# The last two steps' products of an FNet and GELU kernel in two rounds of 128 tokens

## The chip, the core and the metric

The kernel runs on one core of one Trainium2 chip. The metric is the device time of one execution in microseconds (us). The kernel before was run three times: 1854.57, 1856.98 and 1858.54 us, so its median is 1856.98 us. The profile shown here is of one further execution, which took 1857.67 us; the span that it shows, from the first to the last instruction, is 1855.9 us.

The core has five engines with queues of their own: TensorE (PE in the profile, with its weight loads shown as PEld), VectorE (DVE), ScalarE (ACT), GpSimd (POOL) and SyncE (SP). Each works through its instructions in the order in which they were put down. SP and ACT also issue the DMA transfers of this kernel.

## What is computed

```python
def _attn_ref(x):                       # x: (8, 3008, 256) float32
    X = np.fft.fft(x, axis=1)
    X = np.fft.fft(X, axis=2)
    return X.real.astype(np.float32)

def _moe_ref(x, w_in, w_out):           # x: (24064, 256), w_in: (256, 2048), w_out: (2048, 256)
    h = x @ w_in
    g = h * (1.0 / (1.0 + np.exp(-1.702 * h)))
    return (g @ w_out).astype(np.float32)
```

The real part of a two-dimensional Fourier transform of each of the 8 sequences is the input of a two-layer network with a sigmoid GELU. The sequences count 3008 positions of 256 features; the network turns every position (a token) into 2048 hidden values and back into 256.

## The kernel before, in words

The transform along the 3008 = 47 x 64 positions is done in two stages of products with cosine and sine tables, after folding the input on its symmetry; the transform along the features is folded into the first weight matrix (`wcs`). What is left for a token is a pair of products, one with the cosine and one with the sine half, and their sum and difference give the hidden values of a token and of its mirror image at once.

The main loop runs over `steps`, which are tuples of sequence `b` (8), block `blk` (3), half `hh` (2) and step `p` (8, called `NP`). The eight steps of one `(b, blk, hh)` are a group: it deals with 256 pairs of tokens, and each step adds the share of 2 x 128 hidden values to the group's output sums. In a turn `t` of the loop the hidden values of step `t` are made (products on PE into the banks `x`, the activation on ACT, sums on DVE and POOL), and `product(t - LAG, ...)` with `LAG = 3` multiplies those of three steps earlier with the second weight matrix. The program's order on each engine is written out by hand; no planner changes it.

The second product uses a scheme with seven products instead of eight (Strassen's, in Winograd's form) over 2 x 2 blocks: two halves of the hidden values by two halves of the output features, for the token and for its mirror. In the groups between the first and the last, four of the seven are split in the same way once more (`deep(t)`). In the last group, `t >= last`, all seven products are taken whole. Their sums stand in four PSUM banks of 512 columns, of which columns 0 to 255 and 256 to 511 belong to two products: `pot[0]` (bank `o0`), `pot[1]` (bank `o1`), `pot[3]` (bank `po3`) and `pot[2]` (bank `low`, one product only).

Every product is issued by `halves` (line 184 is its matmul) as two instructions, one for the output's partitions 0 to 63 and one for 64 to 127. In the profile each of these fp32 instructions shows as two MATMUL records and two weight loads. The small products of the deep groups are issued at line 678, with 128 columns each.

For the last two steps of the whole program `product` does not issue at once. It keeps the plan of the second last step and then issues the two steps' products interleaved, bank by bank: 4 products into `o0`, 4 into `o1`, 4 into `po3` and 2 into `low`, each with all 256 columns. These are 14 products, 28 instructions and 56 records on PE, and nothing comes behind them there.

Then `combine` closes the group. ACT copies the first product's sum out of `o0` (line 747). DVE adds up the others in SBUF, in `oc` (lines 750, 751, 761 and 756), and `turned` transposes each half (half 0 is the tokens, half 1 their mirror images), 128 x 512 values, into the output tile `os` (line 730). After each of the two transposes `store` issues four DMAs of 64 KB, one for each 32 partitions, in runs of 64 values, which are 256 bytes (line 816). In the last group two of the four are issued by SP and two by ACT; elsewhere all are issued by SP. The group's sums on DVE in order are:

```python
c12 = c11 + pot[0][256:]        # L750, after ACT's copy of c11 = pot[0][:256]
c21 = c12 + pot[1][:256]        # L751
c12, c22' = c12, c21 + pot[1][256:]   # L761, one instruction of 512 columns
c11 += pot[3][:256]; c12 += pot[3][256:]   # L756, then transpose and store of half 0
c21 += pot[2][:256]             # L756, then transpose and store of half 1
```

(The third line stands for one addition into `oc[256:512]` and `oc[512:768]`.)

Of the kernel before, what the change touches and what calls it, by code (L numbers as in the profile page):

```python
# [29 lines left out]
ALU = mybir.AluOpType  # L30
# [10 lines left out]
RUN = 32  # L41
# [5 lines left out]
def view(ap, offset, *dims):  # L47
    return bass.AP(ap.tensor, ap.offset + offset, [list(d) for d in dims])


def free(ap, offset, *dims):
    return bass.AP(ap.tensor, ap.offset + offset, [list(ap.ap[0])] + [list(d) for d in dims])


def kp(u, a):

    n, i = a // 4, 2 * (a % 4) + u
    return 8 * n + i if n else 7 - i
# [54 lines left out]
def kernel(ctx: ExitStack, tc, x, w_in, w_out, tab1, tab2, out):  # L113
    nc = tc.nc
# [12 lines left out]
    op = ctx.enter_context(tc.tile_pool(name="op", bufs=2, space=SB))  # L127
# [25 lines left out]
    big = cv.tile([128, 19 * 1024], F32, tag="big", name="big")  # L153
# [15 lines left out]
    def bank(name, tag=None):  # L169
        if tag is None:  # L170
            tag = spare.pop(0)
            spare.append(tag)
        if tag in ("o0", "o1"):
            return o_banks[int(tag[1])]
        return (rest if tag[0] == "o" else psp).tile([128, 512], F32, tag=tag, name=name)
# [5 lines left out]
    def halves(out, lhs, rhs, **how):  # L181

        for c0 in (0, 64):
            nc.tensor.matmul(out[c0:c0 + 64], lhsT=lhs[:, c0:c0 + 64], rhs=rhs, skip_group_check=True, **how)  # L184
# [323 lines left out]
    NP = NF // 2  # L508
    steps = [(b, blk, hh, p) for b in range(B) for blk in range(NBLK) for hh in range(2) for p in range(NP)]
    vb, ht, xb, gt, pot = {}, {}, {}, {}, {}  # L510
    LEFT, MADE, RIGHT, SUM, RES, OUT = 0, 4096, 8192, 14336, 16384, 18432
    A11, A21, S3, S2 = range(4)
    A12, S4, A22, S1 = range(4)
    oc = big[:, OUT:OUT + 1024].rearrange("p (q n) -> p q n", q=4)
    last = len(steps) - NP

    def width(t):

        return 226 if steps[t][1:3] == (0, 1) else 256
# [26 lines left out]
    def left(t, q, n):  # L546
        return big[:, at_left(t, q):at_left(t, q) + n]

    def right(t, q, n):
        return big[:, at_right(t, q):at_right(t, q) + n]  # L550
# [74 lines left out]
    def deep(t):  # L625

        return NP <= t < last
# [20 lines left out]
    def spot(pair_, k):  # L648
        return 256 + 128 * pair_ if k == 1 else 768 * pair_ + 128 * SPOT[k]

    def both(k, *dims):
        return free((o_banks[1] if k == 1 else pot["low"])[:], spot(0, k), [spot(1, k) - spot(0, k), 2], *dims)
# [37 lines left out]
    def product(t, lo, hi):  # L690

        p, n = steps[t][3], width(t)
        if lo == 0 and p == 0:
            for q in range(2):
                pot[q] = bank(f"po{q}", f"o{q}")
            if t >= NP:
                pot[2] = pot["low"]
            if t >= last:
                pot[3] = bank("po3", "b2")
        if t < NP:  # L700

            h = ht[t]
            plan = [(half, dh, wo[:, p, 2 * f + dh, :], h[:, half, f, :n])
                    for half in range(2) for dh in range(2) for f in range(2)]
        else:
            plan = [(0, 0, wo[:, p, 0, :], left(t, A11, n)), (0, 1, wt[:, p, 0, :], left(t, S2, n)),
                    (1, 0, wt[:, p, 1, :], left(t, S3, n))]
            if not deep(t):
                plan += [(1, 1, wt[:, p, 3, :], right(t, S1, n)), (3, 1, wo[:, p, 3, :], right(t, S4, n)),
                         (3, 0, wo[:, p, 2, :], right(t, A12, n)), (2, 0, wt[:, p, 2, :], right(t, A22, n))]  # L710
        todo = plan[lo:hi]

        if t >= len(steps) - 2:
            if hi:
                return
            pot[t] = plan
            if t == len(steps) - 2:
                return
            todo = [it for pair_ in zip(pot.pop(t - 1), pot.pop(t)) for it in pair_]
        begun = set() if p else pot.setdefault("begun", set())  # L720
        for q, i, lhs, rhs in todo:
            halves(pot[q][:, i * 256:i * 256 + n], lhs, rhs, start=(p == 0 and q not in begun), stop=(p == NP - 1))
            begun.add(q)
        if hi is None and p == 0:
            del pot["begun"]

    def turned(t, o, half, src):

        b, blk, hh, p = steps[t]
        nc.vector.transpose(free(o[:], half * 512, [32, 2], [64, 8], [1, 32]), free(src, (RUN - 1) * half, [256, 2], [RUN, 8], [1 - 2 * half, RUN]))  # L730
        store(b, blk, hh, o, half)

    def combine(t):

        b, blk, hh, p = steps[t]
        if p < NP - 1:
            return
        n = width(t)
        o = pot["out"] = op.tile([128, 4, 256], F32, tag="os", name="os")
        if t < NP:  # L740
            for half in range(2):
                turned(t, o, half, pot[half][:])
            return
        if n < 256:
            nc.gpsimd.memset(oc[:, :, n:], 0.0)
        c11, c12, c21, c22 = (oc[:, q, :n] for q in range(4))
        nc.scalar.copy(c11, pot[0][:, 0:n])
        if deep(t):
            nc.scalar.copy(free(big[:], RES + 1024 + 384, [512, 2], [1, n // 2]), both(1, [1, n // 2]))
        nc.vector.tensor_tensor(c12, c11, pot[0][:, 256:256 + n], op=ALU.add)  # L750
        nc.vector.tensor_tensor(c21, c12, pot[1][:, 0:n], op=ALU.add)  # L751
        if deep(t):
            return
        fifth(free(pot[1][:], 256, [0, 2], [1, n]), n)
        for out_, i1, half in (c11, pot[3][:, 0:n], None), (c12, pot[3][:, 256:256 + n], 0), (c21, pot[2][:, 0:n], 1):
            nc.vector.tensor_tensor(out_, out_, i1, op=ALU.add)  # L756
            if half is not None:
                turned(t, o, half, oc[:, 2 * half:])

    def fifth(m5, n):  # L760
        nc.vector.tensor_tensor(free(oc, 256, [512, 2], [1, n]), oc[:, 1:3, :n], m5, op=ALU.add)  # L761
# [37 lines left out]
    def turn_last(t, half):  # L799

        if group_end(t):
            turned(t, pot["out"], half, oc[:, 2 * half:])

    def store(b, blk, hh, o, half):

        last = (b, blk, hh) == (B - 1, NBLK - 1, 1)
        k0, step = kp(0, 4 * blk), kp(1, 4 * blk) - kp(0, 4 * blk)
        row, by = (NA * (1 + RUN * (1 - hh)) - k0, -step) if half else (NA * RUN * hh + k0, step)
        for q in range(4):
            src = o[32 * q:32 * q + 32, 2 * half:2 * half + 2, :].rearrange("p i n -> p (i n)")  # L810
            eng = nc.scalar if last and q % 2 else nc.sync

            def put(at, k2s, places):
                dst = view(out, (b * S + row + at * by) * D + 64 * q, [NA * D, k2s], [by * D, places], [1, 64])
                part = src[0:k2s, 64 * at:64 * (at + places)]
                eng.dma_start(out=dst, in_=part.rearrange("p (n c) -> p n c", c=64))


            whole = 8 if blk or (hh == 0 and half == 0) else 7
            put(0, RUN, whole)  # L820
            if whole == 7 and (hh, half) != (1, 1):
                put(7, 1 if hh else RUN - 1, 1)
# [106 lines left out]
    n = len(steps)  # L929
# [52 lines left out]
    for t in range(n + LAG):  # L982
        if t < NP:
# [15 lines left out]
            if t >= LAG and t != LAG + 1:  # L999
                product(t - LAG, 0, None)  # L1000
            if t == LAG:
                product(1, 0, None)
# [16 lines left out]
        else:  # L1019
# [14 lines left out]
            if opening:  # L1034
                small_products(*other)
            cut = 0 if opening and not after else 3 if after else 2
            product(t - LAG, 0, cut)
            if after:
                small_products(one[0], one[1][:1])
# [27 lines left out]
        if t >= LAG:  # L1067
            combine(t - LAG)
            combine_last(t - LAG - 2)
            turn_last(t - LAG - 3, 0)  # L1070
            turn_last(t - LAG - 4, 1)
# [32 lines left out]
```

## Time and profile before

| what | value |
|---|---|
| median of three runs | 1856.98 us (1854.57 to 1858.54) |
| profiled execution | 1857.67 us, span 1855.9 us |
| PE busy | 1838.7 us, 99% of the span |
| DVE, ACT, POOL busy | 1514.7, 1151.2 and 971.2 us |
| granted TensorE clock | 0.999 over the span |
| last group of PE records (last two steps) | starts at 1843.91 us, last ends at 1850.12 us |
| last DVE instruction (the second transpose) | 1851.14 to 1851.85 us |
| last DMA packets | between 1854.4 and 1854.6 us |

The profile's page gives busy times and the chain of work that ended last. Its timeline lists instructions in order of time, merged where they are of one kind: start, time until the last of them ended, engine, line, operation, output and inputs, and how many. Records of PE overlap, because matmuls are pipelined; the pace of PE is read from the starts of two neighbouring groups, divided by the number of records. The view by stretches of time gives, for each stretch, the busy time of each engine, the granted clock, the busy share of the DMA engines and what they moved in GB/s.

### The profile page before, as it was taken

Reading aid. Unit: us, or ns where it says so; the run is one execution under the profiler, and the core shown is the slowest. Engines: PE = TensorE matmul, PEld = TensorE weight load, DVE = VectorE, ACT = ScalarE, POOL = GpSimd, SP = SyncE. Lnnn points to the kernel's source line nnn. Section 1 sums busy time; section 2 is a strip of 40 time slices with the busy share of each in tenths; the row PEclk is TensorE's granted clock in tenths of the full one; section 3 lists DMA queues with packets and bytes.
Section 4 is the critical chain, followed back from the end, with each engine's and each line's share of the span. In section 5 each row is a group of like instructions: output and inputs, shape, how many; then the busy total and the mean of one; then the engine's idle time right before and its main releaser. Section 6 shows DMA issues by size and latency. Waiting matters only on the chain.

```text
span 1855.9 us, 56072 instructions
## 1 busy us (share of the span) xinstructions
PE 1838.7 (99%) x23722; PEld 1401.5 (76%) x23722; DVE 1514.7 (82%) x2112; ACT 1151.2 (62%) x2241; POOL 971.2 (52%) x1053
## 2 busy tenths in 40 slices
PE   8999999999999999999999999999999999999998
PEld 4677777777777777777777777777777777778776
DVE  6988778888788877987789878888888888878874
ACT  5756666666666656666566666666666666656663
POOL 4776446744367434773348633476445754434442
PEclk9999999999999999999999999999999999999999
DMA  8821340215012340223302132121411111100111
GB/s 265 196 61 34 84 68 19 72 49 102 19 38 53 73 84 13 51 50 88 59 13 64 45 86 53 18 75 35 103 30 24 36 46 36 30 19 13 23 20 24
DMA packets 149706, 105.31 MB, mean 57 GB/s; under 512 B 106057, under 2 KB 130665, under 8 KB 148896
## 3 DMA queue, kind: packets, MB, share of 16 engines
q1 hardware_dynamic: 146624, 99.68, 23.7%
q8 instruction: 187, 3.06, 0.7%
q10 hardware_dynamic: 2832, 2.05, 0.5%
q14 instruction: 63, 0.52, 0.1%
HBM read 64.41 MB, written 48.05 MB: 61 GB/s over the span
## 4 chain that ended last, share of the span: by engine, by line
PE 90%; DVE 5%; ACT 3%; DMA 1%; issue 1%; DVEq 0%; ACTq 0%
PE x L184 33%; PE o L184 26%; PE low L678 23%; PE o L678 4%; PE ps L255 2%; DVE big L644 2%; PE ps L365 1%; DVE big L779 1%; PE psw L184 1%; DMA xt<-in_x_dram 1%; DVE big L604 1%; ACT x L585 1%; DVE big L622 0%; DMA small<-in_tab_dram 0%; ACT g L597 0%
## 5 line engine op out<-in xcount | busy, mean ns | idle before, releaser
L615 POOL TENSOR_TENSOR big<-big 128x256 f32<-128x256 f32 (+1 forms) x376 | 352.0, 936 | 828.7 <-ACT big L607 676.9
L184 PE MATMUL x<-pq,wcs 128*64 128x256 f32 (+1 forms) x6016 | 769.0, 376 | 1.9 <-ACT g L597 1.6
L644 DVE TENSOR_TENSOR big<-big 128x512 f32<-128x512 f32 (+1 forms) x736 | 618.9, 855 | 23.1 <-PE low L678 4.7
L184 PE MATMUL o<-big,wo 128*64 128x256 f32 (+1 forms) x4800 | 620.8, 375 | 0.1
L184 PEld LDWEIGHTS x<-pq,wcs 128*64 128x64 f32 x6016 | 412.2, 137 | 186.1 <-issue 15.0
L184 PEld LDWEIGHTS o<-big,wo 128*64 128x64 f32 x4800 | 341.8, 137 | 147.8 <-DVE big L622 0.5
L597 ACT ACTIVATE g<-x 128x512 f32<-128x512 f32 (+1 forms) x376 | 221.7, 590 | 369.9 <-PE x L184 368.6
L604 DVE TENSOR_TENSOR big<-g,x 128x512 f32<-128x512 f32 (+1 forms) x376 | 249.9, 665 | 212.8 <-ACT big L600 212.6
L585 ACT ACTIVATE x<-nb,af 128x256 f32<-128x256 f32 (+1 forms) x752 | 352.9, 469 | 76.2 <-DVE pq L372 63.1
L678 PE MATMUL low<-big 128*64 128x128 f32 (+1 forms) x5888 | 382.9, 270 | 0.0
L678 PEld LDWEIGHTS low<-big 128*64 128x64 f32 x5888 | 337.6, 137 | 29.2
L616 POOL TENSOR_TENSOR big<-big 128x256 f32<-128x256 f32 (+1 forms) x376 | 351.5, 935 | 0.0
L600 ACT ACTIVATE big<-x 128x512 f32<-128x512 f32 (+1 forms) x376 | 219.2, 583 | 128.2 <-PE x L184 122.5
L607 ACT ACTIVATE big<-big 128x512 f32<-128x512 f32 (+1 forms) x376 | 231.9, 617 | 46.6 <-DVE big L604 44.4
L678 PE MATMUL low<-big,wo 128*64 128x128 f32 (+1 forms) x2944 | 220.5, 271 | 0.2
L678 PEld LDWEIGHTS low<-big,wo 128*64 128x64 f32 x2944 | 171.3, 137 | 4.5 <-DVE big L644 1.6
L623 DVE TENSOR_TENSOR big<-big 128x512 f32<-128x512 f32 (+1 forms) x188 | 166.6, 886 | 6.5
L622 DVE TENSOR_TENSOR big<-big 128x512 f32<-128x512 f32 (+1 forms) x188 | 137.1, 729 | 6.1 <-POOL big L615 6.1
L779 DVE TENSOR_TENSOR big<-big,low 128x512 f32<-128x512 f32 (+3 forms) x184 | 109.0, 609 | 3.5
L678 PEld LDWEIGHTS o<-big,wo 128*64 128x64 f32 x1472 | 92.3, 137 | 24.9
L678 PE MATMUL o<-big,wo 128*64 128x128 f32 (+1 forms) x1472 | 110.1, 270 | 0.0
L227 POOL TENSOR_TENSOR xt<-xt 111x510 f32<-111x510 f32 x56 | 83.7, 1495 | 4.4
(95 smaller groups left out, 964.5 us busy)
## 6 DMA issues: line engine op xcount, KB each, us to landing
out_dram<-os SPq DMA_DIRECT2D x284, 64.0 KB
t<-Td SPq DMA_DIRECT2D x22, 512.0 KB
Td<-xt SPq DMA_DIRECT2D x56, 192.0 KB
xt<-in_x_dram SPq DMA_DIRECT2D x14, 512.0 KB
xt<-Xr SPq DMA_DIRECT2D x14, 512.0 KB
nb<-Nd SPq DMA_DIRECT2D x23, 256.0 KB
out_dram<-os SPq DMA_DIRECT2D x96, 56.0 KB
Xr<-in_x_dram SPq DMA_DIRECT2D x7, 752.0 KB
```

The costliest lines, as they stand in the source:

```text
L184: nc.tensor.matmul(out[c0:c0 + 64], lhsT=lhs[:, c0:c0 + 64], rhs=rhs, skip_group_check=True, **how)
L585: nc.scalar.activation(x[:, i * 256:i * 256 + n], nbt[b, blk][:, hh * 256:hh * 256 + n], ACTF.Copy, scale=af1[:, f:f + 1])
L597: nc.scalar.activation(two(g[:], n), two(xb[t][:], n), ACTF.Copy, scale=2.0)
L600: nc.scalar.activation(front(t), two(xb[t][:], width(t)), ACTF.Gelu_apprx_sigmoid)
L604: nc.vector.tensor_tensor(back(t), two(gt.pop(t)[:], n), two(xb.pop(t)[:], n), op=ALU.subtract)
L607: nc.scalar.activation(back(t), back(t), ACTF.Gelu_apprx_sigmoid)
L615: eng.tensor_tensor(right(t, S1, n), left(t, A21, n), right(t, A22, n), op=ALU.add)
L616: eng.tensor_tensor(left(t, S3, n), left(t, A11, n), left(t, A21, n), op=ALU.subtract)
L622: eng.tensor_tensor(s2, s1, a11, op=ALU.subtract)
L623: eng.tensor_tensor(s4, a12, s2, op=ALU.subtract)
L644: nc.vector.tensor_tensor(out, i0, i1, op=how)
L678: nc.tensor.matmul(o, lhsT=lhs, rhs=rhs, start=first_in, stop=(p == NP - 2), skip_group_check=True)
```

## The change

For the last two steps the 14 products are issued in two rounds. The first round does all 14 for columns 0 to 127 of the tokens, the second all 14 for columns 128 to 255. `combine` calls a new function, `combine_end`, for the last group. It goes through the same additions twice, with 128 columns each time, and adds `pot[3]` into `c12` ahead of `c11`. `turned` now takes a range of columns and so transposes 128 x 256 values, and `store` issues four DMAs of 32 KB after each such transpose. Nothing changes in any other group.

On PE 56 instructions of 128 columns take the place of 28 of 256. On ACT one copy becomes two, of half the columns, and the four stores become eight: copy, four stores, copy, four stores. On DVE eight instructions become sixteen, all of the first half of the tokens ahead of the second. On SP four stores become eight. POOL's instructions stay as they were.

```diff
         begun = set() if p else pot.setdefault("begun", set())
-        for q, i, lhs, rhs in todo:
-            halves(pot[q][:, i * 256:i * 256 + n], lhs, rhs, start=(p == 0 and q not in begun), stop=(p == NP - 1))
-            begun.add(q)
+        parts = ((0, n),) if t < len(steps) - 2 else ((0, n // 2), (n // 2, n))
+        for c0, c1 in parts:
+            for q, i, lhs, rhs in todo:
+                halves(pot[q][:, i * 256 + c0:i * 256 + c1], lhs, rhs[:, c0:c1], start=(p == 0 and q not in begun),
+                       stop=(p == NP - 1))
+                begun.add(q)
...
-    def turned(t, o, half, src):
+    def turned(t, o, half, src, c0=0, n=256):
 
         b, blk, hh, p = steps[t]
-        nc.vector.transpose(free(o[:], half * 512, [32, 2], [64, 8], [1, 32]), free(src, (RUN - 1) * half, [256, 2], [RUN, 8], [1 - 2 * half, RUN]))
-        store(b, blk, hh, o, half)
+        nc.vector.transpose(free(o[:], half * 512 + 2 * c0, [32, 2], [64, n // RUN], [1, 32]),
+                            free(src, c0 + (RUN - 1) * half, [256, 2], [RUN, n // RUN], [1 - 2 * half, RUN]))
+        store(b, blk, hh, o, half, c0 // RUN, n // RUN)
...
+        if not deep(t):
+            combine_end(t, o)
+            return
         nc.scalar.copy(c11, pot[0][:, 0:n])
...
-        fifth(free(pot[1][:], 256, [0, 2], [1, n]), n)
-        for out_, i1, half in (c11, pot[3][:, 0:n], None), (c12, pot[3][:, 256:256 + n], 0), (c21, pot[2][:, 0:n], 1):
-            nc.vector.tensor_tensor(out_, out_, i1, op=ALU.add)
-            if half is not None:
-                turned(t, o, half, oc[:, 2 * half:])
+
+    def combine_end(t, o):
+
+        n = width(t) // 2
+        for c0 in (0, n):
+            c11, c12, c21 = (oc[:, q, c0:c0 + n] for q in range(3))
+            nc.scalar.copy(c11, pot[0][:, c0:c0 + n])
+            nc.vector.tensor_tensor(c12, c11, pot[0][:, 256 + c0:256 + c0 + n], op=ALU.add)
+            nc.vector.tensor_tensor(c21, c12, pot[1][:, c0:c0 + n], op=ALU.add)
+            nc.vector.tensor_tensor(free(oc, 256 + c0, [512, 2], [1, n]), oc[:, 1:3, c0:c0 + n],
+                                    free(pot[1][:], 256 + c0, [0, 2], [1, n]), op=ALU.add)
+            for out_, i1, half in ((c12, pot[3][:, 256 + c0:256 + c0 + n], None), (c11, pot[3][:, c0:c0 + n], 0),
+                                   (c21, pot[2][:, c0:c0 + n], 1)):
+                nc.vector.tensor_tensor(out_, out_, i1, op=ALU.add)
+                if half is not None:
+                    turned(t, o, half, oc[:, 2 * half:], c0, n)
...
-    def store(b, blk, hh, o, half):
+    def store(b, blk, hh, o, half, n0_=0, count=8):
...
+            if count < 8:
+                put(n0_, RUN, count)
+                continue
```

More of the change, by code (lines that the diff above doesn't have):

```diff
@@ L746, in combine @@
         c11, c12, c21, c22 = (oc[:, q, :n] for q in range(4))
+        if not deep(t):
+            combine_end(t, o)
+            return
         nc.scalar.copy(c11, pot[0][:, 0:n])
-        if deep(t):
-            nc.scalar.copy(free(big[:], RES + 1024 + 384, [512, 2], [1, n // 2]), both(1, [1, n // 2]))
+        nc.scalar.copy(free(big[:], RES + 1024 + 384, [512, 2], [1, n // 2]), both(1, [1, n // 2]))
         nc.vector.tensor_tensor(c12, c11, pot[0][:, 256:256 + n], op=ALU.add)
         nc.vector.tensor_tensor(c21, c12, pot[1][:, 0:n], op=ALU.add)
-        if deep(t):
-            return
-        fifth(free(pot[1][:], 256, [0, 2], [1, n]), n)
-        for out_, i1, half in (c11, pot[3][:, 0:n], None), (c12, pot[3][:, 256:256 + n], 0), (c21, pot[2][:, 0:n], 1):
-            nc.vector.tensor_tensor(out_, out_, i1, op=ALU.add)
-            if half is not None:
-                turned(t, o, half, oc[:, 2 * half:])
+    def combine_end(t, o):
[12 more added lines that the diff above has]
+                    turned(t, o, half, oc[:, 2 * half:], c0, n)
     def fifth(m5, n):
```

## The prediction

> **What bounds the kernel now.** I read the page first: PE is busy for 99% of the span, so what counts is PE's time and what lies ahead of its first and behind its last record. The chain that ended last ends in the products of the last two steps. As the change touches nothing ahead of them (on PE, DVE, ACT, POOL and SP the instructions and their waits are the same up to there), I then read only the last 12 us, in the timeline of the whole core.
>
> ```profile
> span 1855.9 us, 56072 instructions
> PE 1838.7 (99%) x23722; PEld 1401.5 (76%) x23722; DVE 1514.7 (82%) x2112; ACT 1151.2 (62%) x2241; POOL 971.2 (52%) x1053
> 1843.91 3.62 PE L184 MATMUL o<-big,wo 128*64 128x256 f32 x32
> 1845.85 0.37 ACT L747 COPY big<-o 128x256 f32<-128x256 f32 x1 [5.73 <-PE o L184]
> 1846.26 0.42 DVE L750 TENSOR_TENSOR big<-big,o 128x256 f32<-128x256 f32 x1 [3.38 <-ACT big L747]
> 1847.36 1.90 PE L184 MATMUL po<-big,wo 128*64 128x256 f32 x16
> 1847.58 0.42 DVE L751 TENSOR_TENSOR big<-big,o 128x256 f32<-128x256 f32 x1 [0.90 <-PE o L184]
> 1848.03 0.69 DVE L761 TENSOR_TENSOR big<-big,o 128x512 f32<-128x512 f32 x1
> 1849.09 1.03 PE L184 MATMUL low<-big,wo 128*64 128x256 f32 x8
> 1849.31 0.75 DVE L756 TENSOR_TENSOR big<-big,po 128x256 f32<-128x256 f32 x2 [0.58 <-PE po L184]
> 1850.09 0.71 DVE L730 STREAM_TRANSPOSE os<-big 128x512 f32<-128x512 f32 x1
> 1850.73 0.38 DVE L756 TENSOR_TENSOR big<-big,low 128x256 f32<-128x256 f32 x1
> 1850.84 2.01 ACTq L816 DMA_DIRECT2D out_dram<-os  x4
> 1851.14 0.71 DVE L730 STREAM_TRANSPOSE os<-big 128x512 f32<-128x512 f32 x1
> ```
>
> From 1849.31 DVE works without a pause to 1851.85; its last wait is for `po`. Behind it come the stores. The same window read by SP's and ACT's lines alone, and by stretches of 0.2 us, shows how long these take:
>
> ```profile
> L816 SPq DMA_DIRECT2D out_dram<-os x4: 317/384/537, 1850.8 to 1852.2; - x4
> L816 ACTq DMA_DIRECT2D out_dram<-os x4: 373/420/549, 1850.8 to 1852.3; - x4
> 1854.40:1854.60 0.20, 0.00 (x0) 0.00 (x0) 0.00 (x0) 0.00 (x0) 0.00 (x0) 0.50 0.44 90
> 1854.60:1854.80 0.20, 0.00 (x0) 0.00 (x0) 0.00 (x0) 0.00 (x0) 0.00 (x0) 0.50 0.00 0
> ```
>
> The issues take 0.32 to 0.55 us each. The last begins at 1852.30 on ACT, its packets end near 1854.5 (2.2 us later), and the program's close takes 1.4 us from there to 1855.9. So the tail is PE to 1850.1, DVE 1.7 us past that, and 4.05 us of stores and close.
>
> **PE's part.** 56 records of 256 columns become 112 of 128. The pace of the old ones: 32 in 1847.36 - 1843.91 = 3.45 us, 107.8 ns each. The new form stands in the trace at the small products, on the same column halves and with the same kind of weight load:
>
> ```profile
> 1791.99 1.04 PE L678 MATMUL low<-big 128*64 128x128 f32 x16
> 1792.86 0.61 PE L678 MATMUL low<-big,wo 128*64 128x128 f32 x8
> ```
>
> That is 0.87 us for 16, 54.4 ns each: half of 107.8 within 1%. 112 x 54.4 - 56 x 107.8 = +0.05 us. Twice as many weight loads (137 ns each) are hidden at this pace in those rows. The first round ends at 1843.91 + 56 x 0.0544 = 1846.96, the second at 1850.00. A consumer starts 0.22 us behind the end of its bank's records (1847.58 against 1847.36, 1849.31 against 1849.09). So in round one `o0`, `o1`, `po3`, `low` are to be read at 1845.00, 1845.87, 1846.74 and 1847.18, in round two at 1848.05, 1848.92, 1849.79 and 1850.22.
>
> **DVE and ACT, round one.** Additions of 256 and 512 columns take 0.42 and 0.69 us, so by the same slope one of 128 takes 0.28; the transpose of 128x256 is shown at line 372 (0.41); ACT's copy takes 0.37 for 256 and 0.58 for 512 columns (line 263), so 0.26 for 128. Between dependent instructions lie 0.03 us, and two independent ones overlap by some 0.07. Copy to 1845.26, additions to 1846.60, wait for `po3`, two additions 1846.74 to 1847.24, transpose to 1847.68, the addition of `low` to 1847.89, second transpose 1847.92 to 1848.33. All of it lies beside PE's second round and costs nothing.
>
> **The queue that the change adds to.** ACT has, in this order, the copy of round one, its four stores, then the copy of round two. That copy could start at 1848.05, when `o0` is complete, but it stands behind stores that wait for both transposes. I take the issues as long as the tail's own rows have them for 64 KB, 0.38 for the first of a pair and 0.46 for the second, with 0.04 between: the pair of half 0 from 1847.72 to 1848.60, that of half 1 to 1849.53. The copy then runs 1849.57 to 1849.83, 1.5 us late. DVE waits for it with all of round two queued behind.
>
> **DVE, round two.** Additions 1849.87 to 1850.15, 1850.18 to 1850.46 and (pair, 256 columns) 1850.49 to 1850.91; by then `po3` has been ready for over a microsecond, so PE no longer sets anything. Two additions to 1851.44, transpose 1851.47 to 1851.88, addition of `low` to 1852.09, transpose 1852.12 to 1852.53. Before, DVE ended at 1851.85: +0.68 us.
>
> **Stores, round two.** ACT's pair of half 0 runs from 1851.92 to 1852.80 and holds up the pair of half 1: 1852.85 to 1853.23, and the last begins at 1853.27, 0.97 later than before. What comes back is the crowd: 512 KB were in flight at once, now only 256 KB, as round one's stores are through. Four stores of 64 KB alone, of the group before, began their last issue at 1838.05 and had their last packets at 1839.4 to 1839.6, 1.45 us later instead of 2.2. I take 1.45, as the bytes in flight match that row: 1854.72, plus 1.4 of close is 1856.1, so +0.2 us on the span of 1855.9. With 2.2 it would be +0.97. With issues of 0.30 us, as stores of 1 and 31 runs have them (line 816 at 1722 and 1693 us), round two starts 0.49 earlier, the last store at 1852.45, and the sum is -0.6 us. I keep -0.6 and +1.0 as ends.
>
> The Trainium skill, page "DMA: Bandwidth & Descriptors", section "Anatomy of one DMA", speaks against the change here: about 2.0 us of a DMA are fixed (mostly the receipt of the write) and only bytes / 436e9 scales, so 32 KB less saves some 0.08 us of a store. By that rule the last leg would stay at 2.1 us and the sum be an estimated +0.9. The rows of 1.45 and 2.2 us, both for 64 KB, show the company to matter more, so I stay with the row.
>
> **Sum.** The profiled execution took 1857.67 us, 0.7 above the median of 1856.98; its own would become 1857.9. Against the median: 1856.98 + 0.2 = 1857.2 us. That is no change that can be measured: 0.2%, about what a measurement of this kernel can tell from none, are 3.7 us.
>
> **Rivals.**
>
> *ACT's issues are cheap.* If the round-two copy were not held up at all, DVE would go with PE: `o1` at 1848.92, `po3` at 1849.79, second transpose done at 1851.38, last store issued at 1852.12, end 0.9 us before the old one. With issues at 0.30 it is -0.6. For it: smaller stores may take less to issue. Against it: a store of 7 or 8 runs to a partition that follows another such takes 0.44 us and more in the rows of the last 200 us, and 4 runs are nearer to these than to 1. Time 1856.2 (1856.1 to 1856.4).
>
> *A store's issue stalls.* Line 816 on SP shows 234/448/2074 ns as shortest, median and longest of 444 issues; one of four in a row at 1765.42 took 1.19. Before, such a stall at the end of one store delayed only its neighbour; in round one on ACT it would delay DVE's whole second round. Price +0.7 to +1.6 us on top: 1858.3 (to 1858.8). Against it: the same eight issues in 2 us at the end of before stayed under 0.55.
>
> *Weight loads set PE's pace, and the kernel is slower.* Place: the 112 records of the two rounds, each with a weight load of 137 ns. If loads were not hidden, `po3` of round two would be ready at 1843.91 + 104 x 0.137 + 0.22 = 1858.4 instead of 1849.8; as round two reaches it at 1850.94 anyway, the price is 7.4 us: 1864.6. It decides from 65 ns a record on (there `po3` comes later than DVE) and passes 0.2% at about 99 ns. Against it stands the row of 54.4 ns, with as many loads.
>
> *The change brings no overlap.* If round two's products waited for round one's readers, the order of the two would be serial. They carry no wait in the program, and round one's last reader of a bank ends at 1847.89, 0.93 us behind the first round's records; that much more on PE would still have `po3` ready at 1850.72, ahead of DVE: +0.2 us as forecast, 1857.2.
>
> **Chances.** Forecast (queue on ACT against lighter stores, -0.6 to +1.0) 0.68; cheap issues 0.10; a stall or a serial order 0.12, all three within 0.2%: 0.90. Weight loads at PE's pace 0.03, and 0.03 for a shift of the median over 3.7 us upwards, 0.04 downwards, since three runs of the same kernel already differ by 4.0 us: slower 0.06, faster 0.04. The first three span 1856.1 to 1858.8; the runs' own scatter about the median (-2.4, +1.6) widens what will be read to 1854.9 to 1859.1.
>
> **What would show it.** PE: two rounds of 3.05 us, no gap. ACT: the second copy at about 1849.6 behind four issues, and DVE's idle time before its second round put down to that copy (some 1.5 us, after 1848.33). DVE's last transpose at 1852.5. Last packets near 1854.7 and a DMA share that has a first hump from 1848.6. The forecast is wrong if PE's pace is above 65 ns, if the copy starts before 1849, or if the last leg is not 1.45 us.

## The result and the profile after

The changed kernel takes 1858.55 us (median; 1857.47 to 1862.21) where the one before, now in 22 runs, takes 1855.33 us (1854.57 to 1858.82). The medians differ by 3.2 us. Their ratio is 1.0016, with a 95% interval of 1.0009 to 1.0023: slower by less than the 0.2% that the prediction set as its bound, and still clear of no change.

The two profiled spans, 1855.9 and 1856.8 us, differ by 0.9 us only. This is chance ahead of the tail: the products of the last two steps began at 1843.91 us in the execution before and at 1841.62 in the one after, with the same instructions ahead of them. (Two executions of one and the same kernel, e4 and e8 below, begin them at 1844.65 and 1840.95.) From that start to the end of the span it is 1855.9 - 1843.91 = 12.0 us before and 1856.8 - 1841.62 = 15.2 us after. The tail grew by 3.2 us, which is what the medians show. All readings below are taken from that start, called T.

The timeline of the changed kernel, from T on (start, time until the last has ended, engine, line, operation, count, and in brackets the idle time ahead and what ended it; weight loads left out):

```profile
1841.62 1.92 PE L184 MATMUL o<-big,wo 128*64 128x128 f32 x32
1843.36 1.04 PE L184 MATMUL po<-big,wo 128*64 128x128 f32 x16
...
1844.67 1.92 PE L184 MATMUL o<-big,wo 128*64 128x128 f32 x32
1845.76 0.27 ACT L764 COPY big<-o 128x128 f32<-128x128 f32 x1 [7.93 <-PE o L184]
1846.06 0.29 DVE L765 TENSOR_TENSOR big<-big,o 128x128 f32<-128x128 f32 x1 [5.47 <-ACT big L764]
...
1846.42 1.04 PE L184 MATMUL po<-big,wo 128*64 128x128 f32 x16
1846.64 0.29 DVE L766 TENSOR_TENSOR big<-big,o 128x128 f32<-128x128 f32 x1 [0.29 <-PE o L184]
...
1847.29 0.61 PE L184 MATMUL low<-big,wo 128*64 128x128 f32 x8
1847.51 0.49 DVE L771 TENSOR_TENSOR big<-big,po 128x128 f32<-128x128 f32 x2
1848.03 0.45 DVE L733 STREAM_TRANSPOSE os<-big 128x256 f32<-128x256 f32 x1
...
1848.51 1.83 ACTq L831 DMA_DIRECT2D out_dram<-os  x4
1848.68 0.45 DVE L733 STREAM_TRANSPOSE os<-big 128x256 f32<-128x256 f32 x1
1850.38 0.27 ACT L764 COPY big<-o 128x128 f32<-128x128 f32 x1 [4.36 <-DMA out_dram<-os]
1850.68 0.29 DVE L765 TENSOR_TENSOR big<-big,o 128x128 f32<-128x128 f32 x1 [1.55 <-ACT big L764]
...
1852.78 1.85 ACTq L831 DMA_DIRECT2D out_dram<-os  x4
1852.95 0.45 DVE L733 STREAM_TRANSPOSE os<-big 128x256 f32<-128x256 f32 x1
```

PE does what the diff says: 32 records in 1843.36 - 1841.62 = 1.74 us, 54.4 ns each, and the second round starts at T + 3.05. But no engine reads a bank when its first round is through. The first copy is of the first 128 columns of `o0`, complete at T + 0.87 (16 records). It starts at T + 4.14, which is 0.22 us after the 16 records with which round two ends in that bank (1844.67 + 0.87 = 1845.54). The additions follow in the same way: the one of `o1` at 1846.64 and those of `po3` at 1847.51 start 0.22 us after round two has left their banks (1846.42 and 1847.29). So the first half of the sums starts 2.2 us later than the whole ones did (the copy at T + 1.94 before), and the second half stands behind four stores on ACT, as the next copy's line shows. DVE's last instruction ends at T + 11.8 instead of T + 7.9 (1853.40 and 1851.85).

The records of single instructions show why. PE raises the semaphore (the counter on which a reader waits) only four times in these two steps, each time with the last record of round two in a bank (those that start at 1845.44, 1846.32, 1847.19 and 1847.63). The end of round one is not signalled at all, and no reader of the second half carries a wait for PE.

The stretches at the end of the changed kernel (the last two columns are the busy share of the DMA engines and GB/s):

```profile
1855.20:1855.40 0.20, 0.00 (x0) 0.00 (x0) 0.00 (x0) 0.00 (x0) 0.00 (x0) 0.50 0.94 181
1855.40:1855.60 0.20, 0.00 (x0) 0.00 (x0) 0.00 (x0) 0.00 (x0) 0.00 (x0) 0.50 0.24 40
1855.60:1855.80 0.20, 0.00 (x0) 0.00 (x0) 0.00 (x0) 0.00 (x0) 0.00 (x0) 0.50 0.00 0
```

The last store is issued at 1854.17 and its packets are through near 1855.5, 1.35 us later, where it was 2.2 us before.

### The profile page after: what moved, and what is told of

Its sections match the earlier page's. It is cut to its first block, busy times and chain, and to the rows that moved or that the text cites. A ratio compares the mean times of both kernels' runs of the same rounds, so it can differ in the third digit from the quotient of the medians.

```text
span 1856.8 us, 56206 instructions
## 1 busy us (share of the span) xinstructions
PE 1837.4 (99%) x23778; PEld 1403.1 (76%) x23778; DVE 1516.8 (82%) x2120; ACT 1151.1 (62%) x2242; POOL 971.8 (52%) x1053
## 3 DMA queue, kind: packets, MB, share of 16 engines
q8 instruction: 187, 3.06, 0.7%
## 4 chain that ended last, share of the span: by engine, by line
PE 89%; DVE 5%; ACT 2%; DMA 2%; issue 1%; POOL 0%; ACTq 0%; SPq 0%; DVEq 0%; POOLq 0%
PE x L184 32%; PE o L184 25%; PE low L678 23%; PE o L678 4%; DVE big L644 2%; PE ps L255 2%; PE ps L365 1%; DVE big L794 1%; DVE big L604 1%; DMA xt<-in_x_dram 1%; ACT x L585 1%; DVE big L622 1%; DMA Td<-big 0%; ACT g L597 0%; PE po L184 0%
## 5 line engine op out<-in xcount | busy, mean ns | idle before, releaser
L184 PE MATMUL o<-big,wo 128*64 128x256 f32 (+2 forms) x4832 | 621.0, 374 | 0.1
```

## The experiments

Two causes are at hand. Theory A: the readers of round one wait for round two. All products of both rounds stand ahead of all readers in the program, and a reader waits for the last product ahead of it into its bank, whichever columns that writes. Theory B: only ACT's queue costs time, where the second copy stands behind the first half's stores. The trace of the changed kernel shows both at once, so each was undone alone, then both, and then each part of the change was made alone.

**e1: round one's sums written down between the rounds.** The products, sums and stores are the same; only the place of the first half's readers in the program moves.

```diff
                 begun.add(q)
+            if len(parts) > 1:
+                if c0 == 0:
+                    pot["out"] = op.tile([128, 4, 256], F32, tag="os", name="os")
+                combine_end(t, pot["out"], c0)
...
-        for c0 in (0, n):
+        for c0 in (at_,):
```

> The sums, transposes and stores of the first round are written down between the two rounds of products, not behind both; everything else is as in the changed kernel. All times from the start of the first product of the last two steps to the end of the span: 12.0 us before, 15.2 after the change. Theory A (round one's readers wait for the last product into their PSUM bank that stands ahead of them in the program, which in the changed kernel is round two's): the first copy starts at 1.1 us instead of 4.1, the second copy behind ACT's four stores at about 5.7, DVE ends near 8.6, the end is at 12.2 us, so the time falls back to that of before within 0.5 us. Theory B (only ACT's queue, the second copy behind four stores, costs time): the first copy stays at 4.1 and the end at 15.2.

The time is 1855.84 us against 1856.29 of the kernel before, ratio 0.9997 (0.9988 to 1.0006). The loss is gone. T is 1842.52 and the span 1854.8: the tail takes 12.3 us. From e1's timeline:

```profile
1842.52 1.92 PE L184 MATMUL o<-big,wo 128*64 128x128 f32 x32
1843.61 0.27 ACT L767 COPY big<-o 128x128 f32<-128x128 f32 x1 [4.88 <-PE o L184]
...
1845.36 0.48 DVE L774 TENSOR_TENSOR big<-big,po 128x128 f32<-128x128 f32 x2
1845.58 1.92 PE L184 MATMUL o<-big,wo 128*64 128x128 f32 x32
...
1846.36 1.84 ACTq L834 DMA_DIRECT2D out_dram<-os  x4
...
1848.23 0.27 ACT L767 COPY big<-o 128x128 f32<-128x128 f32 x1 [4.35 <-DMA out_dram<-os]
```

PE now raises its semaphore eight times, four times in each round. The first copy starts at T + 1.09 and the second at T + 5.71, behind the stores; `po3` is added at T + 2.84. These are the prediction's own readings (1.09, 5.66 and 2.83), so it describes e1, not the changed kernel. In e1 the products of round two carry a wait for DVE's readers of round one in the same bank, though the columns differ; it costs nothing, since PE's round two starts at T + 3.06, as in the changed kernel (3.05). Theory A holds and B alone does not.

**e2: both copies ahead of ACT's stores**, with the products and their readers where the change has them.

```diff
         for c0 in (0, n):
+            nc.scalar.copy(oc[:, 0, c0:c0 + n], pot[0][:, c0:c0 + n])
+        for c0 in (0, n):
             c11, c12, c21 = (oc[:, q, c0:c0 + n] for q in range(3))
-            nc.scalar.copy(c11, pot[0][:, c0:c0 + n])
```

> The changed kernel with both copies on ACT ahead of the stores; the products' place is not touched. From the start of the last two steps' products to the span's end. Theory A with the queue on top: the first copy still starts at 4.1 us, DVE runs its second half right behind the first (ends near 10.3 instead of 11.8), the end is near 13.6: half of the loss of 3.2 us is left. Theory B: all of it goes, the end is near 12.0.

1856.81 us against 1856.29, ratio 1.0003 (0.9994 to 1.0012), and a tail of 1853.1 - 1839.65 = 13.5 us. From its timeline:

```profile
1839.65 1.92 PE L184 MATMUL o<-big,wo 128*64 128x128 f32 x32
...
1843.80 0.43 ACT L763 COPY big<-o 128x128 f32<-128x128 f32 x2 [7.93 <-PE o L184]
...
1846.71 0.45 DVE L733 STREAM_TRANSPOSE os<-big 128x256 f32<-128x256 f32 x1
1847.08 0.25 DVE L766 TENSOR_TENSOR big<-big,o 128x128 f32<-128x128 f32 x1
```

The copies still wait until T + 4.15, and DVE goes from one half to the next without a pause. The queue was worth 15.2 - 13.5 = 1.7 us; the late start remains.

**e4: both undone.** As e1, and round one's stores are held back until round two's copy has been put down on ACT.

```diff
+                if c0:
+                    nc.scalar.copy(oc[:, 0, c0:c1], pot[0][:, c0:c1])
+                    for kept in held:
+                        store(*kept)
+                    held.clear()
+                combine_end(t, pot["out"], c0)
...
+        if n < 256 and c0 == 0:
+            held.append((b, blk, hh, o, half, c0 // RUN, n // RUN))
+            return
         store(b, blk, hh, o, half, c0 // RUN, n // RUN)
```

> As e1, and on ACT the second round's copy stands ahead of the first round's stores. Theory A and the queue together: first copy at 1.1 us, second at 4.1, DVE waits for po3 of round two (5.9) and ends near 7.5 instead of 7.9 before, last store issued near 8.2, end near 10.8 us: 1.2 us less than before, 0.06%. If something else holds round two, the end stays at 12 or more.

1854.75 us against 1856.29, ratio 0.9991 (0.9982 to 1.0000). The tail is 1855.5 - 1844.65 = 10.9 us. From its timeline:

```profile
1844.65 1.92 PE L184 MATMUL o<-big,wo 128*64 128x128 f32 x32
1845.74 0.27 ACT L778 COPY big<-o 128x128 f32<-128x128 f32 x1 [4.88 <-PE o L184]
...
1848.79 0.27 ACT L731 COPY big<-o 128x128 f32<-128x128 f32 x1 [2.79 <-PE o L184]
1848.85 4.53 ACTq L845 DMA_DIRECT2D out_dram<-os  x8
...
1849.45 1.04 PE L184 MATMUL po<-big,wo 128*64 128x128 f32 x16
...
1850.54 0.48 DVE L785 TENSOR_TENSOR big<-big,po 128x128 f32<-128x128 f32 x2
...
1851.71 0.45 DVE L744 STREAM_TRANSPOSE os<-big 128x256 f32<-128x256 f32 x1
```

Now both copies follow their own rounds (T + 1.09 and T + 4.14), `po3` of round two is added at T + 5.89, 0.22 us after its records end, and DVE ends at T + 7.5. With both undone, two equal rounds do bring overlap: the tail is 1.1 us shorter than before.

**e8: e4 once more**, to see its time against that of before.

> The kernel of e4 once more, for its time against that of before: end at 10.9 us from the start of the products as in e4, 1.1 us or 0.06% less than before.

1854.42 us against 1855.74, ratio 0.9993 (0.9984 to 1.0002), and again 1851.8 - 1840.95 = 10.9 us. Both medians lie 1.3 to 1.5 us lower and the tail repeats exactly, but each interval only just reaches 1; so the shorter tail is shown by the traces, and by the times alone not quite.

**e5: the halves without the rounds.** The products go back to 256 columns; `combine_end` stays as changed.

```diff
-        parts = ((0, n),) if t < len(steps) - 2 else ((0, n // 2), (n // 2, n))
+        parts = ((0, n),)
```

> The changed kernel without the two rounds: products of 256 columns as before, sums, transposes and stores by halves of the tokens as after. Theory A with the queue on top: readers start as in before (first copy at 1.9 us, po3 at 5.4), the second copy waits behind four stores until about 8.3, the end is near 14.7 us: most of the loss stands without any round. If the rounds themselves cost the time: 12.0 us.

1858.69 us against 1856.29, ratio 1.0014 (1.0005 to 1.0022): as slow as the change itself. Its tail is 1855.9 - 1841.18 = 14.7 us, +2.7. The view of who waited for whom in its last 16 us (engine, line and tile, what it waited for, us in total, times, longest):

```profile
ACT big L764 <- DMA out_dram<-os: 6.1, 1, 6.1
ACT big L764 <- PE o L184: 5.7, 1, 5.7
DVE big L765 <- ACT big L764: 4.8, 2, 3.3
```

The first copy starts as early as before (T + 1.94), the second at T + 8.29, behind the stores. With every product in place, splitting the sums into two halves with stores between them costs 2.7 us.

**e6: the rounds without the halves.** The kernel before, with only the loop over `parts` in `product`.

> The kernel before with its products in two rounds, and nothing else changed: sums, transposes and stores of all 256 columns. Theory A: each bank is read when its second round is through, so the first copy starts at 4.1 us after the start of the products instead of 1.9, po3 is read at 5.9 instead of 5.4, DVE ends near 8.7 instead of 8.0, and the end is near 12.7 us against 12.0: rounds alone cost some 0.7 us. If readers went by columns, no reader of 256 columns would come earlier either, so this run prices the rounds under A; under a theory in which rounds cost nothing, 12.0.

1856.43 us against 1855.74, ratio 1.0003 (0.9994 to 1.0012), and a tail of 1854.2 - 1841.48 = 12.7 us, +0.7, with the copy of `o0` at T + 4.15. From its timeline:

```profile
1841.48 1.92 PE L184 MATMUL o<-big,wo 128*64 128x128 f32 x32
...
1845.63 0.37 ACT L750 COPY big<-o 128x256 f32<-128x256 f32 x1 [7.93 <-PE o L184]
...
1847.02 0.69 DVE L764 TENSOR_TENSOR big<-big,o 128x512 f32<-128x512 f32 x1
1847.16 0.61 PE L184 MATMUL low<-big,wo 128*64 128x128 f32 x8
1847.62 0.74 DVE L759 TENSOR_TENSOR big<-big,po 128x256 f32<-128x256 f32 x2
```

The rounds alone cost little. `po3` is complete at T + 5.68 instead of T + 5.18, and the late additions ahead of it delay its own to T + 6.14 (5.9 was expected), against T + 5.40 before.

**e7: e4 with rounds of 160 and 96 columns.**

```diff
-        parts = ((0, n),) if t < len(steps) - 2 else ((0, n // 2), (n // 2, n))
+        parts = ((0, n),) if t < len(steps) - 2 else ((0, 160), (160, n))
```

> The kernel of e4 with a first round of 160 columns and a second of 96. If PE set the end of the second round, a smaller one would end earlier: po3 of round two at 5.9 as in e4, DVE's work behind it 0.3 us shorter, end near 10.5. If DVE sets it (its first round takes longer by a quarter and ends near 5.3), nothing is gained: DVE ends near 7.6 and the end is near 10.9.

1854.78 us against 1855.74, ratio 0.9996 (0.9987 to 1.0004); the tail is 1853.0 - 1841.91 = 11.1 us, 0.2 more than e4. From its timeline:

```profile
1846.72 0.51 DVE L744 STREAM_TRANSPOSE os<-big 128x320 f32<-128x320 f32 x1
1847.03 0.83 PE L184 MATMUL po<-big,wo 128*64 128x96 f32 x16
...
1848.22 0.42 DVE L784 TENSOR_TENSOR big<-big,po 128x96 f32<-128x96 f32 x2
```

Round two's products for `po3` are through near 1847.7, and DVE comes to them at 1848.22: the longer first half holds it up, as the second branch of the expectation has it (it ended 0.2 us later than put there).

The tails side by side:

| kernel | first copy (T +) | second copy (T +) | DVE ends (T +) | end (T +) |
|---|---|---|---|---|
| before | 1.9 | none | 7.9 | 12.0 |
| changed | 4.1 | 8.8 | 11.8 | 15.2 |
| e1, readers between the rounds | 1.1 | 5.7 | 8.9 | 12.3 |
| e2, copies ahead of stores | 4.1 | with the first | 10.1 | 13.5 |
| e4 and e8, both | 1.1 | 4.1 | 7.5 | 10.9 |
| e5, halves alone | 1.9 | 8.3 | 11.3 | 14.7 |
| e6, rounds alone | 4.1 | none | 8.7 | 12.7 |
| e7, 160 and 96 columns | 1.3 | 4.7 | 7.7 | 11.1 |

## Why the prediction was right and where it was wrong

That the change would stay within 0.2% was right (3.2 us of 1855), and 1858.55 lies within 1854.9 to 1859.1. The second is partly luck. The prediction laid this range around 1856.98, the median of three runs, from which it reaches from -2.1 to +2.1 us; the 22 runs give 1855.33 for the kernel before, and the 3.2 us measured from there lie outside those bounds. Nor was it a change that cannot be measured, as its sum has it: the interval of the ratio excludes 1. The forecast of +0.2 us was 3 us too low, and its account of the overlap was wrong. Step by step:

- *PE's part* was right: 54.4 ns a record and the two rounds as timed; hidden weight loads, so the slower rival with PE's pace falls.
- *DVE and ACT, round one* is the step that failed. It has the banks "to be read at 1845.00, 1845.87, 1846.74 and 1847.18", which is 0.22 us behind round one. Measured from T, the first copy should have come at 1.09 and came at 4.14. The row for the 0.22 us showed that a consumer starts behind the last records in its bank, and in the kernel before the bank's last records were also the consumer's own. The step took the second for the first. With the readers between the rounds, in e1, its times come true within 0.05 us.
- *The queue that the change adds to* was right in kind: the second copy stood behind four stores in every version that has this order, and cost 1.7 us in the changed kernel (e2). In the forecast this was nearly paid for by an early first half; as that started 3.05 us late, the whole chain slid by as much: second copy at T + 8.76 instead of T + 5.66.
- *DVE, round two* and *stores, round two* were right in size: 3.0 us from the copy to the last transpose's end (2.7 from the first addition; forecast 2.66), issues of 0.37 to 0.46 us on ACT, and 1.35 us instead of 1.45 from the last issue to the last packet. The 0.85 us that the last leg lost against before came with 256 KB in flight instead of 512 KB: at 256 KB, stores of 64 KB and of 32 KB differ by only 0.1 us (1.45 and 1.35). The Trainium skill, page "DMA: Bandwidth & Descriptors", section "Anatomy of one DMA — SWDGE (gpsimd) path", which the prediction drew on, gives its fixed 2.0 us for DMAs issued by GpSimd, while these stores are issued by SP and ACT. A small share of the size agrees with these rows; a last leg of an estimated 2.1 us does not, and the measured 1.35 decides.
- The rival *the change brings no overlap* had the right order of events, a serial one, by the wrong way and at the wrong price. It looked for products that wait for readers, and priced this at +0.2. What happened is that readers waited for products. The program told it: no reader of the second half carries a wait for PE, which is only possible if the first half's waits have covered round two already. *Cheap issues* and *a stall* fall: the issues were as in the rows of before.

The wait by bank was seen as a fact of how this program's waits are set, from both sides: readers of one half of the columns wait for products into the other half, and in e1 products wait for such readers. A version in which the two would run on one bank at the same time was not tried. The Trainium skill, page "PSUM — Partial Sum Buffer", section "PSUM bank collisions raise a hardware error", asks for guards by bank and 32 partitions rather than by address, because two engines at once in the same bank and the same 32 partitions raise an error, whichever columns they touch; no run here shows that. From these runs alone it stays open whether a wait by columns could be had at all; e1 and e4 show that it isn't needed.

## What to carry to other kernels

When work is cut into rounds so that consumers can start early, look in the new program at what each consumer waits for: here a reader that is written down behind both rounds waits for the last writer of the whole bank, so the readers have to stand between the rounds. Splitting a sum doubles its instructions on every queue that it uses, and on an in-order queue that also issues stores the second half waits for the first half's results; put what the next half needs ahead of those stores. Measure a change in the last microseconds from a common event in the trace: here the start of that event moved by 2.3 us between executions, and hid over two thirds of the effect in the spans.

## What the runs showed of the hardware

Matmul records of 128, 160 and 96 columns kept PE's time for the last two steps nearly unchanged: 6.28 us from T to the end of the last record in the changed kernel and in e7, against 6.21 before. A store of 32 KB took nearly as long to issue on ACT (0.37 to 0.46 us) as one of 64 KB (0.37 to 0.55), so eight stores in place of four held ACT's queue twice, for 1.83 and 1.85 us from the first issue to the end of the last, where four took 2.01.
